# Strided sparse attention with a multiplicative feed-forward: q and k transposes in 64-row halves, joined with the scores of the pair before

## The chip, the cores and the metric

The kernel runs on one core of one Trainium2 chip. The metric is the device time of one execution in microseconds. TensorE (PE) does matmuls and transposes, VectorE (DVE) and ScalarE (ACT) read their results out of PSUM and do the elementwise work, GpSimd (POOL) casts loaded data, SyncE (SP) issues loads.

## The reference, cut to what matters

Eight batches, eight heads, 576 positions, head width 64. Heads 0 to 3 look at the last 32 positions, heads 4 to 7 at all earlier positions that are equal modulo 32. The attention's output, 4608 tokens of 512, goes through a feed-forward with no activation function: two products multiplied with each other, then two more matrices.

```python
scores = scale * np.matmul(q, k.transpose(0, 1, 3, 2))
mask_local = (rel >= 0) & (rel < stride)                       # stride = 32
mask_strided = (rel >= 0) & (pos[None, :] % stride == pos[:, None] % stride)
attn = np.exp(scores - max); attn = attn / (sum + 1e-09)        # masked scores count as nothing
x = np.matmul(attn, v)            # -> 4608 x 512
h = (x @ w1) * (x @ w2) @ w3      # 512 -> 1024 -> 1024
out = h @ w_out                   # 1024 -> 512
```

## The kernel before, in words

**Feed-forward.** w3 and w_out are folded once into one matrix `w34` (`fold_tr` transposes w3 on TensorE, `fold_mm` multiplies). Tokens then go in nine chunks of 512. A chunk has 16 units of four 512-column matmuls in `ab_halves` (`a` fills `aps`, which ACT copies to `asb`; `bb` fills `bps`, which DVE multiplies with `asb` into `abt`) and eight units in `o_halves` (two units per output tile; ACT copies it to `osb` and issues the store). Their outputs take turns on the three buffers of `psF`.

**Attention.** Work goes by pairs of heads, four pairs per batch: `hp` 0 and 1 are local (six chunks of 96 queries), `hp` 2 and 3 strided (eight chunks of 72). The phases of a pair are:

- `ph_T` (L208): eight 128x128 transposes of q and k into one `psM` tile, then one copy into `qT` (always ACT) and one into `kT` (ACT in the first two batches, DVE after that). The two copies read different halves of the tile. Positions 512 to 575 are done for all pairs of a batch at once in `ph_R` (L225), with four transposes and four small copies.
- `ph_S` (L238): two halves of a pair's chunks. Each half has 6 or 8 score matmuls, which alternate between the heads (array rows 0 to 63 and 64 to 127) and write the two halves of a `psB` tile; then exp on ACT (L253) over 576 columns and the mask product on DVE (L255).
- `ph_PV` (L259): for each half 6 or 8 matmuls with v into another `psB` tile. v carries a column of ones, so column 65 of each chunk is the sum of the exps; DVE takes its reciprocal (L274) and multiplies (L276).
- `ph_T2` (L279): six or eight transposes back into a `psM` tile, and a copy into `xT` (ACT, or DVE for local pairs from batch 2 on), from which the feed-forward reads.

**PSUM.** `psF` has 3 buffers, `psB` 2 of double size, `psM` 1, and all eight banks are taken.

**Order.** TensorE's instructions keep the order in which the code writes them (`pe`, L65). The Tile framework derives all waits between the engines from the order in the code, and orders the instructions of the other engines itself. The attention phases are put in a list (`stream`, L377 to L397), and `host` (L400) sets them between the units of the weight fold or of a feed-forward chunk, evenly: batch 0 goes into the fold, batch 1 into the first chunk, batch b into chunk b-1. With the order of before, a batch in the middle has 21 such items among 24 units. `batch_end` marks where a batch must be complete, because the next chunk reads its `xT`.

Loads of q, k and v are issued on SP's queue one to two chunks ahead and cast by POOL (L74, L181, L192).

Of the kernel before, what the change touches and what calls it, by code (L numbers as in the profile page):

```python
# [8 lines left out]
FP32 = mybir.dt.float32  # L9
FP16 = mybir.dt.float16  # L10
AF = mybir.ActivationFunctionType
# [3 lines left out]
def _ap(t: bass.AP, off_add, dims):  # L15
    return bass.AP(tensor=t.tensor, offset=t.offset + off_add, ap=dims)
# [3 lines left out]
def kernel(  # L20
# [11 lines left out]
    nc = tc.nc  # L32
    B, H, S, D = q.shape
# [3 lines left out]
    P = 128  # L37
# [4 lines left out]
    scale = 1.0 / float(D) ** 0.5  # L42
# [6 lines left out]
    SQ, ST = 72, 8  # L49
    NM = 512  # L50
    NR = S - NM
    KW = 640

    consts = ctx.enter_context(tc.tile_pool(name="consts", bufs=1))
    stgp = ctx.enter_context(tc.tile_pool(name="stgp", bufs=9))
    qkp = ctx.enter_context(tc.tile_pool(name="qkp", bufs=2))
    att = ctx.enter_context(tc.tile_pool(name="att", bufs=2))
    ffn = ctx.enter_context(tc.tile_pool(name="ffn", bufs=2))
    psF = ctx.enter_context(tc.tile_pool(name="psF", bufs=3, space=bass.MemoryType.PSUM))
    psB = ctx.enter_context(tc.tile_pool(name="psB", bufs=2, space=bass.MemoryType.PSUM))  # L60
    psM = ctx.enter_context(tc.tile_pool(name="psM", bufs=1, space=bass.MemoryType.PSUM))

    AHEAD = 2

    def pe(ins):  # L65
        return tc.keep_in_program_order(ins)

    def copy(eng, out, in_):
        if eng == "a":
            nc.scalar.copy(out=out, in_=in_)  # L70
        elif eng == "v":
            nc.vector.tensor_copy(out=out, in_=in_)  # L72
        else:
            nc.gpsimd.tensor_copy(out=out, in_=in_)  # L74


    id16 = consts.tile([P, P], FP16)
# [3 lines left out]
    maskL = consts.tile([P, LQ], FP16)  # L81
# [16 lines left out]
    maskS = consts.tile([SQ, SQ], FP16)  # L98
# [9 lines left out]

    qT = consts.tile([P, 4, S], FP16)
    kT = consts.tile([P, 4, KW], FP16)  # L110
    ptms = [consts.tile([P, 640], FP16, name=f"ptm{i}") for i in range(4)]
    nc.vector.memset(kT[:, 0:2, 0:32], 0.0)
    nc.vector.memset(kT[:, 2:4, S:KW], 0.0)
    for i in range(2):
        nc.vector.memset(v16L[i][:, :, :, D], 1.0)
        nc.vector.memset(v16L[i][0:32, :, 0, :], 0.0)
        nc.vector.memset(v16S[i][:, :, :, D], 1.0)
    for i in range(4):
        nc.vector.memset(ptms[i][:, 576:640], 0.0)

    xT = [consts.tile([P, NTOK], FP16, name=f"xT{cc}") for cc in range(4)]
    w1h = consts.tile([P, KM, DF], FP16)
# [31 lines left out]
    x16 = {}  # L154
# [43 lines left out]
    pairs = []  # L198
    for b in range(B):
        for hp in range(4):  # L200
            s = Pair()
            s.b, s.hp, s.local = b, hp, hp < 2
            s.w, s.n = (LQ, LT) if s.local else (SQ, ST)
            s.kr = P if s.local else SQ
            s.ptm, s.xqs = {}, {}
            pairs.append(s)

    def ph_T(s):  # L208
        ps = psM.tile([P, 2, NM], FP16, tag="m")
        for i, nm in enumerate("qk"):  # L210
            src = x16[(s.b, nm, s.hp // 2)]
            h0 = 2 * (s.hp % 2)
            for c in range(4):
                pe(nc.tensor.transpose(ps[:, i, c * P:(c + 1) * P],  # L214
                                       src[:, c, h0:h0 + 2].rearrange("p h d -> p (h d)"), id16))
        for i, (eng, t) in enumerate((("a", qT), ("a" if s.b < AHEAD else "v", kT))):
            if s.local:
                c0 = 32 * i
                copy(eng, t[:, s.hp, c0:c0 + NM].rearrange("x (p c) -> x p c", c=4),
                     ps[:, i].rearrange("x (c p) -> x p c", c=4))  # L220
            else:
                copy(eng, t[:, s.hp, 0:S].rearrange("x (u c w) -> x u c w", u=2, c=4)[:, :, :, 0:64],
                     ps[:, i].rearrange("x (c t u) -> x u c t", c=4, u=2))

    def ph_R(b):  # L225
        ps = psM.tile([P, 4, 2, 128], FP16, tag="m")
        pv = ps.rearrange("x g a w -> x (g a w)")[:, 0:512].rearrange("x (g a w) -> x g a w", g=4, a=2)
        src = x16[(b, "r")]
        for g in range(4):
            pe(nc.tensor.transpose(pv[:, g].rearrange("x a w -> x (a w)"),  # L230
                                   src[:, 2 * g:2 * g + 2].rearrange("p h d -> p (h d)"), id16))
        for i, (eng, t) in enumerate((("a", qT), ("a" if b < AHEAD else "v", kT))):
            c0 = 32 * i + NM
            copy(eng, t[:, 0:2, c0:c0 + NR], pv[:, 0:2, i])
            copy(eng, t[:, 2:4, 0:S].rearrange("x g (c w) -> x g c w", w=SQ)[:, :, :, 64:SQ],
                 pv[:, 2:4, i].rearrange("x g (s c) -> x g c s", c=ST))

    def ph_S(s):  # L238
        w, kr = s.w, s.kr
        m = s.n // 2  # L240
        for g in range(2):
            sps = psB.tile([P, 2, 512], FP32, tag="big")
            for i in range(m):
                t = g * m + i
                ks = w * t
                for h in range(2):
                    r = bass.ds(64 * h, 64)
                    pe(nc.tensor.matmul(sps[:, h, i * w:(i + 1) * w], kT[r, s.hp, ks:ks + P],  # L248
                                        qT[r, s.hp, ks:ks + w], start=True, stop=True))
            pte = att.tile([P, 2, 288], FP16, tag="pte", bufs=3)  # L250
            ptm = ptms[(2 * s.hp + g) % 4]
            s.ptm[g] = ptm
            nc.scalar.activation(out=pte[0:kr], in_=sps[0:kr, :, 0:288], func=AF.Exp, bias=0.0, scale=scale)  # L253
            mk = maskL if s.local else maskS
            nc.vector.tensor_mul(ptm[0:kr, 0:576].rearrange("p (a x) -> p a x", x=w),  # L255
                                 pte[0:kr].rearrange("p h (a x) -> p (h a) x", x=w),
                                 _ap(mk, 0, [[mk.ap[0][0], kr], [0, s.n], [1, w]]))

    def ph_PV(s, g):  # L259
        w, kr = s.w, s.kr  # L260
        m = s.n // 2
        ptm = s.ptm[g]
        vt = (v16L if s.local else v16S)[s.b % 2]
        xps = psB.tile([P, 2, 512], FP32, tag="big")
        for i in range(m):
            for h in range(2):
                c0 = h * 288 + i * w
                pe(nc.tensor.matmul(xps[:, h, i * 65:(i + 1) * 65], ptm[0:kr, c0:c0 + P],  # L268
                                    vt[0:kr, 2 * (s.hp % 2) + h, g * m + i, :], start=True, stop=True))
        rcp = att.tile([P, 2, 4], FP32, tag="rcp")  # L270
        xqs = att.tile([P, 4, 2, D], FP16, tag="xqs", bufs=4)
        s.xqs[g] = xqs
        xv = xps[0:w, :, 0:m * 65].rearrange("p h (i e) -> p h i e", e=65)
        nc.vector.reciprocal(out=rcp[0:w, :, 0:m], in_=xv[:, :, :, D])  # L274
        rp = rcp.ap[0][0]
        nc.vector.tensor_mul(xqs[0:w, 0:m].rearrange("p i h d -> p h i d"), xv[:, :, :, 0:D],  # L276
                             _ap(rcp, 0, [[rp, w], [4, 2], [1, m], [0, D]]))

    def ph_T2(s):  # L279
        w, n = s.w, s.n  # L280
        m = n // 2
        ps = psM.tile([P, 1024], FP16, tag="m")
        for t in range(n):
            pe(nc.tensor.transpose(ps[:, t * w:(t + 1) * w],  # L284
                                   s.xqs[t // m][0:w, t % m].rearrange("p h d -> p (h d)"),
                                   id16[0:w, 0:w]))
        o = xT[s.hp][:, S * s.b:S * s.b + S]
        if s.local:
            copy("a" if s.b < AHEAD else "v", o, ps[:, 0:S])
        else:  # L290
            nc.scalar.copy(out=o.rearrange("x (p c) -> x p c", c=n),  # L291
                           in_=ps[:, 0:S].rearrange("x (c p) -> x p c", p=w))
# [78 lines left out]
    stream = []  # L371
    batch_end = {}

    def add(f, *a):
        stream.append(lambda: f(*a))

    for b in range(B):  # L377
        if b < AHEAD:
            add(ph_T, pairs[4 * b])
            add(ph_R, b)  # L380
            add(ph_T, pairs[4 * b + 1])
        for i in range(4):
            p = 4 * b + i
            add(ph_S, pairs[p])
            if i or b >= AHEAD:
                add(ph_T2, pairs[p - 1])
                if i == 0:
                    batch_end[b - 1] = len(stream)
            add(ph_PV, pairs[p], 0)
            if i == 3 and AHEAD <= b + 1 < B:  # L390
                add(ph_R, b + 1)
            add(ph_PV, pairs[p], 1)
            if i < 2 or AHEAD <= b + 1 < B:
                add(ph_T, pairs[p + 2])
        if b + 1 < AHEAD or b == B - 1:
            add(ph_T2, pairs[4 * b + 3])
            batch_end[b] = len(stream)  # L397
    pos = [0]

# [38 lines left out]
    for jc in range(KF):  # L438
        h0, h1 = fold_mm(jc)
# [59 lines left out]
```

## Time and profile before

| what | value |
|---|---|
| three runs | 295.0, 295.15, 292.44 us, median 295.0 |
| profiled execution | span 299.8 us, from the first to the last instruction; no other time of it is given |
| TensorE clock granted, mean | 0.989 |
| DMA | 48.64 MB, mean 162 GB/s |
| weight fold with batch 0 | about 22 to 49 us |
| chunk 0 with batch 1 | about 49 to 85 us |
| chunks 1 to 6 with batches 2 to 7 | about 85 to 249 us |
| chunks 7 and 8, no attention beside | to the end |

How to read the profile: a line of the timeline has the start, the length, the engine, the line of the code, the operation, `out<-in`, the shapes and the number of instructions that were merged. Matmuls overlap one another, so what a group takes from TensorE is read from its start to the start of the next group; the length also holds the last matmul's own passage. In square brackets stands the time for which the engine was idle ahead of the line and what ended it. A line of the waits has who waited for whom, the total in us, how many times, and the longest.

### The profile page before, as it was taken

Reading aid. Unit: us, or ns where it says so; the run is one execution under the profiler, and the core shown is the slowest. Engines: PE = TensorE matmul, PEld = TensorE weight load, DVE = VectorE, ACT = ScalarE, POOL = GpSimd, SP = SyncE. Lnnn points to the kernel's source line nnn. Section 1 sums busy time; section 2 is a strip of 40 time slices with the busy share of each in tenths; the row PEclk is TensorE's granted clock in tenths of the full one; section 3 lists DMA queues with packets and bytes.
Section 4 is the critical chain, followed back from the end, with each engine's and each line's share of the span. In section 5 each row is a group of like instructions: output and inputs, shape, how many; then the busy total and the mean of one; then the engine's idle time right before and its main releaser. Section 6 shows DMA issues by size and latency. Waiting matters only on the chain.

```text
span 299.8 us, 6132 instructions
## 1 busy us (share of the span) xinstructions
PE 268.9 (90%) x2401; PEld 141.6 (47%) x2401; DVE 174.6 (58%) x353; ACT 147.1 (49%) x269; POOL 102.1 (34%) x118
## 2 busy tenths in 40 slices
PE   2258898989889989989999899999999999999995
PEld 1025554435545545545555445555555555444442
DVE  2011775357888866886789659747765774340430
ACT  2025586557565545536645554564455445333332
POOL 5539744486626724653455345110000000000000
PEclk9996999999999999999999999999999999999999
DMA  7999999999869929994896796030012002003003
GB/s 228 349 160 352 288 348 258 216 273 209 249 200 243 242 79 270 246 178 159 240 236 140 253 193 164 27 115 2 2 57 87 0 2 105 35 2 116 24 2 140
DMA packets 58653, 48.64 MB, mean 162 GB/s; under 512 B 29184, under 2 KB 49664, under 8 KB 58624
## 3 DMA queue, kind: packets, MB, share of 16 engines
q1 hardware_dynamic: 53440, 38.81, 54.7%
q10 hardware_dynamic: 5184, 9.44, 8.7%
q8 instruction: 19, 0.31, 0.5%
q14 instruction: 10, 0.08, 0.1%
HBM read 38.80 MB, written 9.44 MB: 161 GB/s over the span
## 4 chain that ended last, share of the span: by engine, by line
PE 67%; DVE 9%; DMA 9%; ACT 9%; issue 3%; SPq 1%; POOL 0%; ACTq 0%
PE ops L335 19%; PE bps L321 18%; PE aps L312 16%; PE xps L268 4%; PE ps L214 4%; DMA st<-in_moe_w_dram 4%; ACT pte L253 3%; DVE ptm L255 3%; DMA st<-in_moe_w_out_dram 3%; DMA out_dram<-osb 3%; PE sps L248 2%; PE ps L284 2%; DVE abt L323 2%; ACT xT L291 2%; DVE kT L72 2%
## 5 line engine op out<-in xcount | busy, mean ns | idle before, releaser
L312 PE MATMUL aps<-xT,w1h 128*128 128x512 f16 x288 | 75.3, 379 | 3.2 <-ACT xT L291 3.0
L323 DVE TENSOR_TENSOR abt<-bps,asb 128x512 f16<-128x512 f32 x72 | 49.5, 687 | 47.2 <-PE bps L321 45.5
L321 PE MATMUL bps<-xT,w2h 128*128 128x512 f16 x288 | 74.0, 379 | 0.0
L315 ACT COPY asb<-aps 128x512 f32<-128x512 f32 x72 | 42.2, 586 | 64.6 <-PE aps L312 61.8
L335 PE MATMUL ops<-w,abt 128*128 128x512 f16 x288 | 71.7, 379 | 0.5 <-DVE abt L323 0.5
L74 POOL CAST t<-st 128x1024 f16<-128x1024 f32 (+1 forms) x48 | 47.4, 991 | 43.4 <-DMA st<-in_k_dram 29.1
L253 ACT ACTIVATE pte<-sps 128x576 f16<-128x576 f32 (+1 forms) x64 | 38.4, 650 | 7.3 <-PE sps L248 7.1
L276 DVE TENSOR_TENSOR xqs<-xps,rcp 96x384 f16<-96x384 f32 (+1 forms) x64 | 39.6, 619 | 2.0
L321 PEld LDWEIGHTS <-w2h 128*128 128x128 f16 x288 | 25.8, 97 | 31.6 <-issue 5.1
L70 ACT COPY qT<-ps 128x512 f16<-128x512 f16 (+1 forms) x48 | 22.9, 481 | 29.9 <-PE ps L214 23.8
L346 ACT COPY osb<-ops 128x512 f32<-128x512 f32 x36 | 21.1, 586 | 29.9 <-PE ops L335 28.6
L335 PEld LDWEIGHTS <-abt 128*128 128x128 f16 x288 | 24.7, 98 | 23.1 <-DVE abt L323 1.0
L312 PEld LDWEIGHTS <-w1h 128*128 128x128 f16 x288 | 25.1, 98 | 22.2
L181 POOL CAST v16L<-st 32x768 f16<-32x768 f32 (+1 forms) x32 | 27.1, 847 | 18.4 <-DMA st<-in_v_dram 12.6
L268 PEld LDWEIGHTS <-ptm 72*128 72x128 f16 (+1 forms) x448 | 21.4, 97 | 19.2 <-DVE ptm L255 6.4
L255 DVE TENSOR_TENSOR ptm<-pte,maskL 128x576 f16<-128x576 f16 x32 | 20.5, 646 | 11.7 <-ACT pte L253 11.2
L72 DVE COPY kT<-ps 128x512 f16<-128x512 f16 (+1 forms) x36 | 18.8, 535 | 10.1 <-ACT qT L70 10.0
L255 DVE TENSOR_TENSOR ptm<-pte,maskS 72x576 f16<-72x576 f16 x32 | 19.6, 620 | 8.5 <-ACT pte L253 7.9
L192 POOL CAST v16S<-st 72x1024 f16<-72x1024 f32 x16 | 16.9, 1055 | 20.1 <-PE xps L268 11.4
L335 PE MATMUL ops<-woh,w3T 128*128 128x512 f16 x64 | 19.8, 440 | 3.2 <-POOL woh L74 3.1
L214 PEld LDWEIGHTS <-t 128*128 128x128 f16 x256 | 17.1, 99 | 8.8 <-issue 2.6
L214 PE MATMUL ps<-id,t 128*128 128x128 f16 x256 | 20.1, 222 | 0.5 <-POOL t L74 0.5
(48 smaller groups left out, 175.8 us busy)
## 6 DMA issues: line engine op xcount, KB each, us to landing
out_dram<-osb ACTq DMA_DIRECT2D x36, 256.0 KB, 2.0
st<-in_moe_w_dram SPq DMA_DIRECT2D x16, 512.0 KB, 8.9
st<-in_q_dram SPq DMA_DIRECT2D x16, 512.0 KB, 5.5
st<-in_k_dram SPq DMA_DIRECT2D x16, 512.0 KB, 6.6
st<-in_v_dram SPq DMA_DIRECT2D x32, 144.0 KB, 6.1
st<-in_v_dram SPq DMA_DIRECT2D x16, 256.0 KB, 7.2
st<-in_moe_w_out_dram SPq DMA_DIRECT2D x4, 512.0 KB, 8.5
st<-in_q_dram SPq DMA_DIRECT2D x8, 128.0 KB, 8.1
```

The source lines that it names most:

```text
L74: nc.gpsimd.tensor_copy(out=out, in_=in_)
L181: nc.gpsimd.tensor_copy(out=vt[pr, hs, :, 0:D], in_=st[pr])
L214: pe(nc.tensor.transpose(ps[:, i, c * P:(c + 1) * P], src[:, c, h0:h0 + 2].rearrange("p h d -> p (h d)"), id16))
L253: nc.scalar.activation(out=pte[0:kr], in_=sps[0:kr, :, 0:288], func=AF.Exp, bias=0.0, scale=scale)
L255: nc.vector.tensor_mul(ptm[0:kr, 0:576].rearrange("p (a x) -> p a x", x=w), pte[0:kr].rearrange("p h (a x) -> p (h a) x", x=w), _ap(mk, 0, ...
L268: pe(nc.tensor.matmul(xps[:, h, i * 65:(i + 1) * 65], ptm[0:kr, c0:c0 + P], vt[0:kr, 2 * (s.hp % 2) + h, g * m + i, :], start=True, stop=T ...
L276: nc.vector.tensor_mul(xqs[0:w, 0:m].rearrange("p i h d -> p h i d"), xv[:, :, :, 0:D], _ap(rcp, 0, [[rp, w], [4, 2], [1, m], [0, D]]))
L312: pe(nc.tensor.matmul(aps, w1h[:, ci, bass.ds(jc * P, P)], xT[ci][:, tok], start=(ci == 0), stop=(ci == KM - 1)))
L315: nc.scalar.copy(out=asb, in_=aps)
L321: pe(nc.tensor.matmul(bps, w2h[:, ci, bass.ds(jc * P, P)], xT[ci][:, tok], start=(ci == 0), stop=(ci == KM - 1)))
L323: nc.vector.tensor_mul(abts[tch][:, jc, :], bps, st["asb"])
L335: pe(nc.tensor.matmul(st["ps"], lhs(ci), rhs(ci), start=(ci == 0), stop=(ci == KF - 1)))
```

## The change

- The transposes of q and k become 16 instead of 8, each of 64 rows: the halves of the rows (`u`) alternate and write the two halves of a tile `pt`. The 64 last positions (`rest`), once per batch, are eight further transposes in the same tile; `ph_R` is gone.
- A new phase `ph_TS` (the block) writes the transposes of the next pair, its q and k copies, then all scores of the present pair, then the copies of the rest.
- The scores go into one tile `sps` (columns 0 to 511 of each half), except for the last chunk of each head, which goes into columns 384 and up of `pt`, beside the transposes. The first score of a block in the code is that of head 0's last chunk.
- exp and mask run once over what lies in `sps` (2 x 480 or 2 x 504 columns) and once over what lies in `pt` (2 x 96 or 2 x 72).
- PV has groups of three chunks: two groups for local pairs, three (3, 3, 2) for strided ones. All but the last write into the halves of `sps`; the last takes a `psM` tile.
- Strided pairs' q and k copies are split by the half of the tile.
- `psB` (4 banks) is replaced by `psA` and `psT`, one buffer of 2 banks each. `psM` serves T2 and the last PV group.
- A batch in the middle now has 18 items among the 24 units: (block, T2, PV0, PV1) twice and (block, T2, PV0, PV1, PV2) twice.

```diff
+    NB = 512
+    LC = 384
-    psB = ctx.enter_context(tc.tile_pool(name="psB", bufs=2, space=bass.MemoryType.PSUM))
+    psA = ctx.enter_context(tc.tile_pool(name="psA", bufs=1, space=bass.MemoryType.PSUM))
+    psT = ctx.enter_context(tc.tile_pool(name="psT", bufs=1, space=bass.MemoryType.PSUM))
...
+            s.n1 = NB // s.w
+            s.groups = [list(range(g, min(g + 3, s.n))) for g in range(0, s.n, 3)]
...
+    def ph_T(s, rest, pt):
+        ps = pt.bitcast(FP16)
+        h0 = 2 * (s.hp % 2)
         for i, nm in enumerate("qk"):
             src = x16[(s.b, nm, s.hp // 2)]
             for c in range(4):
+                c0 = i * 256 + c * 64
+                for u in range(2):
+                    r = half_rows(u)
+                    pe(nc.tensor.transpose(ps[:, u, c0:c0 + 64],
+                                           src[r, c, h0:h0 + 2].rearrange("p h d -> p (h d)"), id16[r, r]))
+        if rest:
...
+        engs = (("a", qT), ("a" if s.b < AHEAD else "v", kT))
+        for i, (eng, t) in enumerate(engs):
+            pi = ps[:, :, i * 256:i * 256 + 256]
             if s.local:
                 c0 = 32 * i
+                copy(eng, t[:, s.hp, c0:c0 + NM].rearrange("x (u p c) -> x u p c", u=2, c=4),
+                     pi.rearrange("x u (c p) -> x u p c", c=4))
             else:
+                to = t[:, s.hp, 0:S].rearrange("x (v c w) -> x v c w", v=2, c=4)
+                for u in range(2):
+                    copy(eng, to[:, :, :, 32 * u:32 * u + 32],
+                         pi[:, u].rearrange("x (c t v) -> x v c t", c=4, v=2))
...
+    def ph_S(s, pt):
+        w, kr, n, n1 = s.w, s.kr, s.n, s.n1
+        sps = psA.tile([P, 2, NB], FP32, tag="a", name="sps")
+        s.ps = sps
+
+        def sc(h, c):
+            r = half_rows(h)
+            o = sps[:, h, c * w:(c + 1) * w] if c < n1 else pt[:, h, LC:LC + w]
+            pe(nc.tensor.matmul(o, kT[r, s.hp, w * c:w * c + P], qT[r, s.hp, w * c:w * c + w],
+                                start=True, stop=True))
+
+        for i in range(n):
+            sc(0, (i - 1) % n)
+            sc(1, i)
+        pte = att.tile([P, 2 * S], FP16, tag="pte", bufs=2)
+        ptm = s.ptm = ptms[s.hp % 2]
+        mk = maskL if s.local else maskS
+        m1 = 2 * n1 * w
+        for lo, hi, src in ((0, m1, sps[0:kr, 0:2, 0:n1 * w]), (m1, 2 * S, pt[0:kr, :, LC:LC + w])):
+            nc.scalar.activation(out=pte[0:kr, lo:hi], in_=src, func=AF.Exp, bias=0.0, scale=scale)
+            nc.vector.tensor_mul(ptm[0:kr, lo:hi].rearrange("p (a x) -> p a x", x=w),
...
+        if g < len(s.groups) - 1:
+            xps = s.ps[:, g]
+        else:
+            pv2 = psM.tile([P, NB], FP32, tag="m", name="pv2")
+            xps = pv2[:, :]
...
+    def ph_TS(t, s):
+        pt = psT.tile([P, 2, NB], FP32, tag="t")
+        after = ph_T(t, t.hp == 0, pt) if t is not None else (lambda: None)
+        if s is not None:
+            ph_S(s, pt)
+        after()
+
+    for p, s in enumerate(pairs):
+        b, i = divmod(p, 4)
+        if i == 0 and b < AHEAD:
+            add(ph_TS, s, None)
+        nxt = pairs[p + 1] if p + 1 < len(pairs) else None
+        if nxt is not None and nxt.hp == 0 and nxt.b < AHEAD:
+            nxt = None
+        add(ph_TS, nxt, s)
+        if i or b >= AHEAD:
+            add(ph_T2, pairs[p - 1])
...
+        for g in range(len(s.groups)):
+            add(ph_PV, s, g)
+        if i == 3 and (b + 1 < AHEAD or b == B - 1):
+            add(ph_T2, s)
             batch_end[b] = len(stream)
```

## The prediction

> **What bounds the kernel now.** I read the page first (engines, clock, chain), then the stages, the order of time around one pair, and last the waits.
>
> ```profile
> span 299.8 us, 6132 instructions
> PE 268.9 (90%) x2401; PEld 141.6 (47%) x2401; DVE 174.6 (58%) x353; ACT 147.1 (49%) x269; POOL 102.1 (34%) x118
> PE 67%; DVE 9%; DMA 9%; ACT 9%; issue 3%; SPq 1%; POOL 0%; ACTq 0%
> ```
>
> TensorE is the bound: 67% of the chain that ended last. Busy time alone says less, so the stages:
>
> ```profile
> 22.40:49.20 26.80, 23.30 (x268) 14.60 (x269) 15.88 (x35) 18.27 (x34) 17.58 (x18) 0.89 1.06 324
> 66.80:84.50 17.70, 15.27 (x200) 8.87 (x197) 13.74 (x29) 11.83 (x24) 10.20 (x11) 1.00 0.97 216
> 190.60:218.50 27.90, 27.60 (x275) 14.94 (x272) 18.49 (x41) 15.15 (x28) 1.04 (x1) 1.00 0.11 39
> ```
>
> The columns are PE, PEld, DVE, ACT and POOL busy, then the clock. From about 84 us on PE leaves almost nothing (27.60 of 27.90); there a change is worth what it adds to or takes from PE's own queue. At 22 to 49 us (batch 0 beside the weight fold) and 58 to 84 us (batch 1) PE waits for the chain score, exp, mask, PV. One local pair of the dense part, PE, ACT and DVE in turn:
>
> ```profile
> 204.32 0.61 PE L214 MATMUL ps<-id,t 128*128 128x128 f16 x8
> 204.77 1.03 PE L312 MATMUL aps<-xT,w1h 128*128 128x512 f16 x4
> 205.73 0.43 PE L248 MATMUL sps<-qT,kT 64*128 64x96 f16 x12
> 206.09 1.04 PE L321 MATMUL bps<-xT,w2h 128*128 128x512 f16 x4
> ...
> 204.97 0.58 ACT L70 COPY qT<-ps 128x512 f16<-128x512 f16 x1 [0.91 <-PE ps L214]
> 205.59 0.69 DVE L72 COPY kT<-ps 128x512 f16<-128x512 f16 x1 [0.30 <-ACT qT L70]
> ```
>
> PE time is read from start to start: T 0.45 us, scores 0.36, and 0.09 before them (204.77 + 0.864 for the unit of four matmuls ahead is 205.64). The kT copy starts only when the qT copy ends, though the two read different halves of `ps`. The waits say that this is the rule:
>
> ```profile
> DVE kT L72 <- ACT qT L70: 10.0, 19, 1.2
> ACT w3T L360 <- DVE w3T L359: 15.9, 5, 8.7
> PE ps L284 <- DVE kT L72: 2.2, 4, 1.0
> ```
>
> In the first two lines engines take turns on one PSUM tile while reading disjoint columns. So the program orders users of such a tile by place, not by bytes. In the third, T2 waits for T's copies, as both use `psM`.
>
> **The change, part by part.** A unit is four 512-column matmuls, 0.864 us by the starts above 51 us (51.17, 52.03, 52.90). Let e be the end of the unit ahead of a block.
>
> *Transposes.* 8 of 128 columns took 0.45. How 64-row halves run is shown by the scores, which already alternate halves: 16 of 72 columns take 0.43 including 0.20 of the last one's own time, so 15.6 ns each; 64 columns should do no worse, 16 x 14.5 = 0.23. I take 0.23; if the halves did not overlap, 16 x 29 = 0.47. Gain 0.22 per pair. R (4 of 128, 0.225) becomes 4 more pairs, 0.117. The 0.09 and some 0.1 behind the scores are paid once either way. The Trainium skill (TensorE: Matmul & The Clock Gate, Wait — 56ns, not 53.3ns?) gives a floor of about 25 ns from start to start for small matmuls; by it T would take 0.40 and 30 blocks 5 us more. This trace disagrees, with 15.6 ns.
>
> *The new wait, which decides.* `pt` holds the transposes and the last score chunk in the same two halves, other columns. In the code the q and k copies come before the scores, PE keeps its written order, and the first score written, `sc(0, n-1)`, goes into `pt`. By the rule seen above it waits for both copies. Behind it on PE stand all scores and the next units; ACT's exp, DVE's mask and PV wait in turn. Today nothing waits so: T writes for a pair that comes later and a unit fills the gap.
> Local, k on DVE: from the first T matmul to the end of kT were 206.28 - 204.32 = 1.96 (other pairs 1.95 to 2.0); T ends 0.17 sooner (last start 0.39 to 0.22), so 1.79. PE resumes 0.05 later (84.43 after a copy that ended at 84.38). So scores start at e + 0.09 + 1.84 = e + 1.93, and the next unit 0.36 later at e + 2.29. Before: 0.45 + 0.09 + 0.36 = 0.90. Cost **1.38** net of the gain; with R's move, 0.117 - 0.225, **1.27**.
> Strided: copies are split by half. ACT 128x512 is 587 ns, 128x128 269, so 256 columns 375; DVE 689 and 228, so 382. From T's start: q0 0.48 to 0.855, k0 0.89 to 1.27, k1 to 1.65. The first score needs half 0 only (1.32), the last half 1 (1.70): next unit at e + 1.92, cost **1.01**; if it waits for all copies, 1.24. No row shows which; the code's order (h=0 tail first, h=1 tail last) fits the first, so I take 1.01.
> The Trainium skill (PSUM — Partial Sum Buffer, PSUM bank collisions raise a hardware error) tells one to guard PSUM by bank and quadrant, not by address. The kT and w3T waits agree; guarded by address, the sum would be that of the third rival.
>
> *exp and mask.* exp 657 ns for 576 columns; at the copies' 0.83 ns a column 976 and 338 for 960 and 192, the same in all, but the first part ends 0.32 later. Mask (mean 646, quiet 0.45, crowded 1.06 at 64.01) by width: 1.08 (0.75 to 1.77). PV0 is ready at scores + 0.34 + 0.98 + 0.05 + 1.08 = 2.45. In the dense part 18 items now share 24 units (21 before): three units and a T2 stand between, 0.36 + 2.59 + 0.26 = 3.2, hidden; behind the first strided pair only two, 2.35 against 2.6 with its later second half: 0.25 x 6 batches = **1.5** (0 to 5).
>
> *T2 of the last pair* sits behind one unit; its xT copy queues on ACT behind both exps and an osb: scores + 2.75, against PE's fourth aps matmul at 2.13: 0.6 for today's 0.30, five times: **1.5**.
>
> *Third PV group, split copies.* Strided pairs get one more reciprocal and product (recip. 3 x 0.18 for 2 x 0.20; products 0.554 twice + 0.423 for 2 x 0.685: 0.29) and split copies (ACT 0.16, DVE 0.08): 16 x 0.37 = 6 us on DVE, 3 on ACT. DVE is at 18.5 of 27.9: hidden, 0 to 1.
>
> *PSUM.* T leaves `psM`, so T2 no longer waits for kT: **-2.2**, 1.04 of it inside batch 1. Single `psA`: the next scores come over two units after the last PV that writes there: 0. R moves some 3.5 us ahead; its cast was ready (batch 4's at 131.7, scores at 133.97). No DMA moves; SP's and POOL's order stays.
>
> *Batches 0 and 1.* Here PE already waits and the items stand one unit apart, so I walk the chain by hand with the same terms. The cycle from pair 1 to pair 2 in batch 0: block begins 33.7; T done and copies on ACT from 34.15 (before batch 2 kT is copied there too, parts 0.27 apart); k0 ends 35.05, scores 35.1 to 35.45; exp after the last copy 35.65 to 36.6; mask with POOL beside it 1.2 and a little ahead of it, 38.0; PV0, a unit, PV1, a unit; next block 40.3, scores 41.7: 6.6 us. Before, the halves followed each other and the copies were done in the gaps: 33.81 to 39.52, 5.7. Walked so, the scores of pairs 0 to 3 start at 29.2, 35.1, 41.7, 47.7 (before 28.64, 33.81, 39.52, 43.65), and the batch ends at 53.3 for 49.2: **+4.1**. Bounds +1 (the wait falls wholly into time in which PE waits) and +7 (it adds wholly, with longer masks).
> Batch 1, from T at 58.08 to the first aps behind its T2 at 84.68, was 26.6. After, from the same point: a lone T block with the rest, whose six ACT copies hold the single `psT` until 2.4; T 2.5, scores of pair 4 at 4.05, of 5 at 10.95, of 6 at 17.0, of 7 at 24.4 (R's transposes in it), pair 8's block ends 31.7, T2 32.0: **+5.4**, pair 8's wait included. Bounds +2 and +8, by the same reasons.
>
> **Sum.** Pairs 9 to 30: 5 local at 1.38, 12 strided at 1.01, 5 with R at 1.27 = 25.4. With 1.5 + 1.5 - 1.2 = 27.2. With 4.1 + 5.4: +36.7. The profiled execution is shown only as its span, 299.8, 4.8 over the median 295.0 of the runs; I add to the median: **332 us**. Bounds: low, nothing for PV0 and xT and +3 for both early batches, 295 + 25.4 - 1.2 + 3 = 322; high, split copies waited for whole (12 x 0.23 = 2.8), PV0 +5 and early batches +15: 295 + 25.4 + 2.8 + 5 + 1.5 - 1.2 + 15 = 343.
>
> **Rivals.**
> - *Copies start late.* When T is done ACT may be in an asb or osb copy (197.33: qT only at 197.81) or DVE in abt; 0.48 in half of the 30 blocks is +7: 339; in all of them with whole-tile waits, 350. Against: units ahead of the blocks are mostly bps, which leave ACT free. 0.12.
> - *Halves don't overlap.* 30 x 0.24 = +7: 339. Against: scores. 0.08.
> - *No wait* (other side). If the scores into `pt` do not wait, T and R give 30 x 0.22 + 7 x 0.11 = 7.4 and psM 2.2; the early batches cost 3.5 and the strided PV0 and xT 4, as exp stands behind the copies: 295 - 9.6 + 7.5 = 293. It decides where the wait per block is under 0.3 us. For it: no row shows a matmul held by a reader of other columns. Against: kT and w3T, 24 waits in all, none seen to overlap. 0.08.
> - *Early batches absorb it.* Their +9.5 falls to 0, as PE waits there anyway: 322. Against: the wait lies on their chain too. 0.10.
> My forecast 0.62, 322 to 343 by itself.
>
> **How the numbers follow.** The likeliest is 332. The range 318 to 345 holds it, the early-batch case and most of the two at 339, leaving out the no-wait case and the 350 end: about 0.15. About 1% is what a measurement of this kernel can tell from no change. Only the no-wait case is not slower: half of it (0.04) faster by over 1%, half (0.04) within 1%, the rest 0.92 slower.
>
> **What would show it.** PE's scores waiting for DVE kT (ACT kT in the first two batches), 1 to 1.5 us each, 30 times; one batch of the dense part 32 to 33 us for 27.9, PE busy nearer 0.85; transposes at about 15 ns from start to start; T2's wait on kT gone; xT's wait about doubled. It is wrong if scores start within 0.2 us of the last transpose.

## The result, and the profile after

The changed kernel takes 349.8 us (median of four runs, 347.5 to 350.3) against 295.1: a ratio of 1.184, interval 1.177 to 1.192. Times of a kernel are medians of its fast runs from here on; runs more than 1.5% above the fastest of the same kernel are left out. I had forecast 332 with a range of 318 to 345. The direction and the cause were right, the size was not: +54.7 us where the sum had +36.7.

The page of the changed kernel: span, engines, granted clock by slice, chain.

```profile
span 348.5 us, 6789 instructions
PE 274.6 (79%) x2689; PEld 138.5 (40%) x2689; DVE 170.3 (49%) x395; ACT 148.8 (43%) x289; POOL 101.1 (29%) x118
PEclk9998999879989999989989999999999999999999
PE 63%; ACT 12%; DVE 9%; DMA 7%; issue 6%; POOL 1%; SPq 1%; ACTq 0%; DVEq 0%
```

PE's share fell from 90% to 79%, no other engine's share rose, and ACT's share of the chain rose from 9% to 12%: the added time is PE waiting. PEclk has more eights than before, which becomes important below. The waits name what PE waits for:

```profile
PE pt L267 <- DVE kT L76: 37.5, 24, 2.1
PE pt L267 <- ACT kT L74: 7.5, 6, 1.3
PE sps L297 <- DVE xqs L305: 2.8, 5, 1.1
```

24 + 6 = 30 waits, one for each block that has transposes and scores, 45.0 us together. The line `PE ps <- DVE kT` of before is gone, as forecast. One block in a quiet stretch, with the transposes and copies of a strided pair:

```profile
242.89 0.41 PE L226 MATMUL pt<-id,t 64*128 64x64 f16 x16
...
243.34 0.65 ACT L74 COPY qT<-pt 128x256 f16<-128x256 f16 x2 [0.81 <-PE pt L226]
244.02 0.76 DVE L76 COPY kT<-pt 128x256 f16<-128x256 f16 x2 [0.26 <-ACT qT L74]
...
244.83 0.21 PE L267 MATMUL pt<-qT,kT 64*128 64x96 f16 x1 [1.53 <-DVE kT L76]
244.83 0.42 PE L267 MATMUL sps<-qT,kT 64*128 64x96 f16 x10
...
245.19 1.04 PE L340 MATMUL aps<-xT,w1h 128*128 128x512 f16 x4
```

Read downward: the 16 transposes, both q copies, then both k copies, and only after the end of the second of them (244.77) the first score. DVE had nothing else to do: it stood idle for 0.26 us and took the first k copy at 244.02, after the end of the second q copy (243.98) and not after that of the first (243.71). From first transpose to first score 1.94 us, of which PE idles 1.53.

A second profile of the kernel before (the run e0, below) had a span of 295.4; stage by stage, by the starts of the first `aps` of each chunk:

| stage | before (e0) | after | difference | forecast |
|---|---|---|---|---|
| to chunk 0 (fold, batch 0) | 46.4 | 53.1 | +6.8 | +4.1, end at 53.3 |
| chunk 0 (batch 1) | 36.1 | 45.0 | +8.9 | +5.4 |
| chunks 1 to 6 (batches 2 to 7) | 167.5 | 204.8 | +37.3 | +27.2 |
| chunks 7 and 8 | 45.4 | 45.5 | +0.1 | 0 |

### The profile page after: what moved, and what is told of

It reads as the page before. It is cut to its first block, busy times and chain, and to the rows that moved or that the text cites. A ratio compares the mean times of both kernels' runs of the same rounds, so it can differ in the third digit from the quotient of the medians.

```text
span 348.5 us, 6789 instructions
## 1 busy us (share of the span) xinstructions
PE 274.6 (79%) x2689; PEld 138.5 (40%) x2689; DVE 170.3 (49%) x395; ACT 148.8 (43%) x289; POOL 101.1 (29%) x118
## 3 DMA queue, kind: packets, MB, share of 16 engines
q1 hardware_dynamic: 53440, 38.81, 45.5%
## 4 chain that ended last, share of the span: by engine, by line
PE 63%; ACT 12%; DVE 9%; DMA 7%; issue 6%; POOL 1%; SPq 1%; ACTq 0%; DVEq 0%
PE bps L349 18%; PE aps L340 17%; PE ops L363 16%; DVE kT L76 5%; ACT qT L74 4%; DMA st<-in_moe_w_dram 3%; PE sps L297 3%; ACT pte L278 2%; PE pt L226 2%; DMA st<-in_moe_w_out_dram 2%; PE pt L267 2%; PE sps L267 2%; DVE ptm L279 2%; PE ps L312 2%; ACT kT L74 1%
## 5 line engine op out<-in xcount | busy, mean ns | idle before, releaser
L349 PE MATMUL bps<-xT,w2h 128*128 128x512 f16 x288 | 77.5, 393 | 0.0
L351 DVE TENSOR_TENSOR abt<-bps,asb 128x512 f16<-128x512 f32 x72 | 49.7, 690 | 54.7 <-PE bps L349 53.7
L78 POOL CAST t<-st 128x1024 f16<-128x1024 f32 (+1 forms) x48 | 47.0, 986 | 43.6 <-DMA st<-in_k_dram 27.7
L267 PE MATMUL pt<-qT,kT 64*128 64x96 f16 (+1 forms) x64 | 12.8, 199 | 45.0 <-DVE kT L76 37.5
L278 ACT ACTIVATE pte<-sps 128x960 f16<-128x960 f32 (+1 forms) x32 | 31.7, 989 | 34.9 <-PE pt L267 34.5
L297 PEld LDWEIGHTS <-ptm 72*128 72x128 f16 (+1 forms) x448 | 24.4, 100 | 28.8 <-DVE ptm L279 8.3
L74 ACT COPY qT<-pt 128x256 f16<-128x256 f16 (+2 forms) x64 | 23.2, 403 | 22.4 <-PE pt L226 16.5
L267 PEld LDWEIGHTS <-kT 64*128 64x128 f16 x448 | 11.2, 95 | 49.1 <-issue 26.7
L279 DVE TENSOR_TENSOR ptm<-pte,maskL 128x960 f16<-128x960 f16 (+1 forms) x32 | 15.4, 523 | 29.8 <-ACT pte L278 29.8
L279 DVE TENSOR_TENSOR ptm<-pte,maskS 72x1008 f16<-72x1008 f16 (+1 forms) x32 | 16.3, 543 | 23.3 <-ACT pte L278 23.0
L305 DVE TENSOR_TENSOR xqs<-sps,rcp 72x384 f16<-72x384 f32 (+1 forms) x48 | 26.6, 554 | 1.6
L76 DVE COPY kT<-pt 128x256 f16<-128x256 f16 (+2 forms) x48 | 19.8, 441 | 13.0 <-ACT qT L74 13.0
```

The costliest lines, as they stand in the source:

```text
L267: pe(nc.tensor.matmul(o, kT[r, s.hp, w * c:w * c + P], qT[r, s.hp, w * c:w * c + w], start=True, stop=True))
L278: nc.scalar.activation(out=pte[0:kr, lo:hi], in_=src, func=AF.Exp, bias=0.0, scale=scale)
L279: nc.vector.tensor_mul(ptm[0:kr, lo:hi].rearrange("p (a x) -> p a x", x=w), pte[0:kr, lo:hi].rearrange("p (a x) -> p a x", x=w), _ap(mk, 0 ...
L297: pe(nc.tensor.matmul(xps[:, o0:o0 + 65], s.ptm[0:kr, c0:c0 + P], vt[0:kr, 2 * (s.hp % 2) + h, c, :], start=True, stop=True))
L349: pe(nc.tensor.matmul(bps, w2h[:, ci, bass.ds(jc * P, P)], xT[ci][:, tok], start=(ci == 0), stop=(ci == KM - 1)))
L351: nc.vector.tensor_mul(abts[tch][:, jc, :], bps, st["asb"])
```

## The experiments

**e0_before_again**: the kernel before, with no edit, for its profile.

> The kernel of before, unchanged, for a second profile: the first had a span of 299.8 us while its four runs took 292.4 to 296.6. If that profiled execution was itself a long one (a 1.77 us wait of PE for xT behind a store at 171 us), this one should have a span of 291 to 296 and no such wait. If profiling lengthens the span, it is again near 300.

It ran in 297.1 us with a span of 295.4, so an execution's time is its span and 1.7 us. The first profile of before (299.8) was therefore an execution of some 301.5 us, longer than any of the runs; batch 0 ended in it at 49.2, here at 46.4. PE's longest wait for xT is 1.4 us here, for 1.8 there.

**e1_copies_last**: the change, with the q and k copies written behind the scores.

```diff
+        def qk_out():
             for i, (eng, t) in enumerate(engs):
...
         def rest_out():
+            qk_out()
...
-        return rest_out if rest else (lambda: None)
+        return rest_out if rest else qk_out
```

> The change with the q and k copies written behind the scores, nothing else moved. Theory (the scores' writes into pt wait for the copies that read pt): the 45 us for which PE stood idle ahead of the scores (37.5 until DVE kT, 7.5 until ACT kT) go, and with them most half-clock stretches (5 to 7 us); exp no longer stands behind the copies. 293 to 302 us, no wait of scores for kT in the profile. Rival (the large exp and mask, the single psA and the third PV group make it slower, and the wait is only where it shows): still over 325, with PE waiting for masks or xqs instead.

306.3 us (305.7 to 308.8; 308.8 is also the median of all five runs), ratio to before 1.033 (1.027 to 1.040). The place of two copies in the code is worth 43.6 of the 54.7 us. No score waits for kT any more. The time stayed above the 293 to 302 expected, and PE shows two other waits, of which the first grew from the 2.8 us of the changed kernel:

```profile
PE sps L299 <- DVE xqs L307: 10.9, 14, 3.1
PE aps L342 <- ACT xT L321: 6.8, 8, 1.7
```

PV's second group for strided pairs writes half 1 of `sps` and waits until DVE has read the first group out of half 0. I had put the single `psA` at zero.

**e2_tails_last**: the change, with the scores in plain order, so that both scores that go into `pt` come last.

```diff
         for i in range(n):
-            sc(0, (i - 1) % n)
+            sc(0, i)
             sc(1, i)
```

> The change with the scores in plain order, so that both scores that go into pt are the last two of a block instead of the first and the last. Theory (only a write into pt waits): the other 10 or 14 scores start within 0.3 us of the last transpose, only the last two wait, as long as before minus some 0.2 us; 30 blocks x 0.2 = 6 us: 341 to 347. Rival (scores wait because copies write qT and kT, which they read): the first score waits as before and the time stays at 348 to 351.

334.9 us (333.3 to 337.7), ratio 1.132 (1.124 to 1.141), 14.9 us less. A block with a strided pair's copies:

```profile
207.03 0.41 PE L226 MATMUL pt<-id,t 64*128 64x64 f16 x16
...
207.28 0.39 PE L267 MATMUL sps<-qT,kT 64*128 64x72 f16 x14
...
208.97 0.21 PE L267 MATMUL pt<-qT,kT 64*128 64x72 f16 x2 [1.30 <-DVE kT L76]
```

14 scores read `qT` and `kT` while the copies write other parts of them, and start 0.25 us after the first transpose; only the two that write into `pt` wait. That settles the place of the wait. The gain was more than twice what I expected. An undisturbed chunk fell from 33.9 to 32.9, that is 0.25 in each of four blocks. The two profiled executions differ by 12.5 us (348.5 and 336.0): 7.8 in chunks 1 to 6, of which 22 x 0.25 = 5.5 are the blocks; 4.1 in chunk 0; 0.6 in batch 0. In chunks 0 to 6 the halved clock, of which more below, comes in two stretches of 3.4 us where the change has five.

**e3_full_rows_q_k_apart**: the change with full transposes, q into half 0 of `pt` and k into half 1, one copy each.

```diff
-                c0 = i * 256 + c * 64
-                for u in range(2):
...
+                pe(nc.tensor.transpose(ps[:, i, c * P:(c + 1) * P],
+                                       src[:, c, h0:h0 + 2].rearrange("p h d -> p (h d)"), id16))
...
-            pi = ps[:, :, i * 256:i * 256 + 256]
+            pi = ps[:, i, 0:NM]
```

> The change with the 8 full 128-row transposes of before instead of the 16 halves, q into half 0 of pt and k into half 1, and single copies, still ahead of the scores. If users take turns by half (bank) of the tile, kT on DVE no longer waits for qT: from the first transpose to the scores about 1.4 us instead of 1.84 and 1.94, some 0.5 us in each of 23 blocks: 338 to 343. If they take turns by the whole tile: first transpose to scores about 2.1, 0.2 us more in each of 30 blocks: 352 to 357.

346.3 us (341.8 to 346.9), ratio 1.165 (1.155 to 1.175), between the two forecasts, so its time decides little. Its rows decide:

```profile
226.51 0.61 PE L223 MATMUL pt<-id,t 128*128 128x128 f16 x8
...
227.16 0.58 ACT L74 COPY qT<-pt 128x512 f16<-128x512 f16 x1 [0.85 <-PE pt L223]
227.77 0.69 DVE L76 COPY kT<-pt 128x512 f16<-128x512 f16 x1 [1.29 <-ACT qT L74]
228.52 0.20 PE L262 MATMUL pt<-qT,kT 64*128 64x96 f16 x1 [1.40 <-DVE kT L76]
```

DVE stands idle for 1.29 us, and kT still starts behind the end of qT (227.74), though the two now read different halves of the tile. So users take turns by the whole tile. From first transpose to score 2.01 us, as the second theory had it (about 2.1). That the time did not rise fits the clock: the profiled execution (341.8 us) has no stretch of halved clock in chunks 1 to 6, where that of the change has three, and takes 201.6 us there for 204.8, though its quiet chunk is longer (34.1 for 33.9).

**e4_copies_last_two_psA**: e1, with the scores in two tiles, one per head, and the large exp as two instructions.

```diff
-    psA = ctx.enter_context(tc.tile_pool(name="psA", bufs=1, space=bass.MemoryType.PSUM))
+    psA = ctx.enter_context(tc.tile_pool(name="psA", bufs=2, space=bass.MemoryType.PSUM))
...
-        sps = psA.tile([P, 2, NB], FP32, tag="a", name="sps")
-        s.ps = sps
+        sps = s.ps = [psA.tile([P, NB], FP32, tag="a", name=f"sps{h}") for h in range(2)]
...
```

> The change with the copies behind the scores (308.8 us in the run before) and, besides, psA as two separate tiles, one for each head, so that exp of the large part is two instructions again. Theory (users take turns by whole tile, so PV's second group waits until DVE has read the first one's half): the 10.9 us of PE waiting for DVE xqs go; ACT has 32 more fixed costs of some 0.16 us, off the path: 297 to 303 us. Rival (the second group is late for its masks anyway): the wait moves to DVE ptm and the time stays at 306 to 310.

298.1 us (294.8 to 299.1), ratio 1.005 (1.000 to 1.010), 8.1 us less than e1 (10.0 by the spans of the profiled executions, 307.0 and 297.0), for a wait of 10.9. As much memory and the same columns: what counts as one tile has changed, and that exp is two instructions. PE's wait of a second PV group for DVE xqs is no longer among the waits; the scores wait for xqs 1.6 us in two places.

**e5_copies_behind_T2**: e4, with the q and k copies one item later, behind T2's copy.

```diff
+    def ph_T2c(s, cur):
+        ph_T2(s)
+        cur.after()
...
-            add(ph_T2, pairs[p - 1])
+            add(ph_T2c, pairs[p - 1], s)
```

> As e4_copies_last_two_psA, with the q and k copies one item later, behind T2's copy. Theory (the 6.8 us of aps waiting for ACT's xT copy are the q copy and both exps that stand ahead of it on ACT): the wait falls from 0.9 to about 0.4 us in each of six chunks, and kT no longer stands ahead of masks and xT on DVE: 3 to 5 us under e4, 292 to 299. Rival (the exps alone make xT late): within 1 us of e4.

296.4 us (293.0 to 297.4; 297.0 over all ten runs), ratio 1.000 (0.995 to 1.006): level with before. The wait of `aps` for xT fell in the quiet chunks from 0.94 to 0.44 us, as expected. The time fell by 1.7 us and not by 3 to 5, and even that cannot be told from the spread of the two kernels.

**e6_change_with_filled_wait**: the change, with 16 matmuls of the identity, which compute nothing that is used, between transposes and scores.

```diff
+                fill = psF.tile([P, 512], FP32, tag="f", name="fill")
+                for i in range(16):
+                    pe(nc.tensor.matmul(fill[:, 0:P], id16, id16, start=True, stop=True))
             ph_S(s, pt)
```

> The change with 16 matmuls of the identity (128 columns, some 0.9 us) between the transposes and the scores of each of the 30 blocks, into a psF buffer that nobody reads: work that computes nothing, put into time in which PE waits for the copies. Theory (part of what my sum lacked is the TensorE clock: 4 half-clock stretches of 3.4 us more than before, brought on by the idle time): PE is no longer idle for long, the clock stays at 0.985 or more, and the time falls by 3 to 8 us, 342 to 347, though work was added. Rival (the clock drops come from elsewhere or cost nothing): clock 0.97 and the time stays at 349 to 352 or rises.

341.5 us (340.2 to 344.2), ratio 1.150 (1.141 to 1.159): 8.3 us less than the change, with 480 matmuls more. The clock of the profiled execution:

```profile
core 0: 340.0 us, clock 0.995
```

It is 0.969 in the changed kernel. The blocks themselves did not become shorter: from first transpose to first score the 22 of chunks 1 to 6 take 43.2 us together in the change and 43.1 here. So PE's idle time cost twice: itself, and the clock behind it.

**e7_masks_per_head**: e5, with the large mask also as one instruction per head.

```diff
-        for lo, hi in ((0, m1), (m1, 2 * S)):
+        for lo, hi in ((0, m1 // 2), (m1 // 2, m1), (m1, 2 * S)):
```

> As e5_copies_behind_T2 (297.0 us), with the large mask also as two instructions, one per head, so that the first runs beside the second exp. Theory (what is left of PE's waits for DVE ptm, 7.8 us in 11 places, is the one large mask that starts only when both exps are done): PV's first group is ready some 0.25 to 0.5 us sooner; 293 to 296 us. Rival (those waits are POOL slowing DVE, or lie in the early batches behind other work): within 1 us of 297.

295.4 us (293.0 to 296.8), ratio 0.997 (0.994 to 1.001): not told apart from before, nor surely from e5. The waits for masks went from 7.8 us in 11 places to 6.8 in 7. In chunks 1 to 6 they fell from 1.1 to 0.2; all the others lie in the early batches, as the rival had it. By stage this last kernel differs from before even so: its profiled execution takes 163.4 us for chunks 1 to 6 where e0 takes 167.5, and 84.7 for 82.5 up to there.

**e8_full_rows_without_the_wait**: e5 with the 8 full transposes in place of the 16 halves (the transposes and single copies as in e3).

> As e5_copies_behind_T2, with the 8 full 128-row transposes of before in place of the 16 halves and single copies for strided pairs. It measures the gain of the halves by itself, where nothing waits behind them. By my term, 0.21 to 0.22 us in each of 30 blocks: 6.5 us more than e5, 302 to 305, and in the profile 0.45 us from the first transpose to the next group instead of 0.24. If the gain is lost in waits elsewhere: within 2 us of 297.

297.6 us (295.7 to 299.95), ratio 1.007 (1.002 to 1.011). One block here, and one of e5:

```profile
209.19 0.61 PE L223 MATMUL pt<-id,t 128*128 128x128 f16 x8
209.73 0.43 PE L263 MATMUL sps<-qT,kT 64*128 64x72 f16 x14
```

```profile
207.56 0.41 PE L226 MATMUL pt<-id,t 64*128 64x64 f16 x16
207.80 0.42 PE L268 MATMUL sps<-qT,kT 64*128 64x72 f16 x14
```

Here 8 transposes and the change to half rows take 0.54 us to the next group, where the 16 halves of e5 take 0.24 and the change to half rows, 0.09 us, stands ahead of them: 0.21 a block, my term. A quiet chunk takes 27.9 us against 27.04 in e5, four times 0.21; but the medians are only 1.2 apart, not 6.5, and the intervals of the two ratios overlap. The gain is seen in the quiet chunks and not shown in the whole time.

## Why the prediction was wrong in size and right in cause

**Right: the step that decides.** "The new wait, which decides" named the place (the first score into `pt`), what ends it (kT on DVE, on ACT in the first two batches) and the count of 30. e2 shows the place, e1 the price. Local blocks were forecast at 1.84 us from first transpose to first score and measured 1.81 (235.10 to 236.91); with the rest 1.96 and 1.93 (225.73 to 227.66). The transposes took 0.24 us for 16, forecast 0.23. Batch 0's end, walked by hand, was 53.3 and is 53.1; that it fits so well is luck, as the account below shows.

**Wrong: the strided block, "cost 1.01; if it waits for all copies, 1.24".** I let users take turns by half of the tile, on the ground that the order of the tails fitted it; even the other end let k's first half start behind q's first. By whole tile both k copies wait for both q copies: 1.94 us to the first score where I had 1.32, and 2.41 from the end of the unit ahead to the next unit (217.28 to 219.69) where I had 1.92. Twelve blocks in chunks 1 to 6: 0.49 x 12 = 5.9 us. The rows of before showed turns inside one buffer of `psM`, a single bank, so they could not tell bank from tile; but nothing in them spoke for halves. e3 shows the whole tile directly.

**Wrong: copies that start late.** In six of the twelve strided blocks of chunks 1 to 6 a copy was late: in four DVE was held by a copy of v or a product (145.85 to 148.21 is 2.36 us), in two ACT by an `asb` copy (2.08 and 2.09). Together 1.2 us over the 1.94. This was part of the first rival, at a smaller price; that the rival's far end, 350, is the measured time is chance, as it took some 14 us for late copies.

**Missing: the clock.** No term had it: I priced PE's idle time at its own length. The profile has it in the windows and in the matmuls; here the four full chunks from 98 us on and, by the order of time, one block after a wait of 1.95 us:

```profile
98.10:133.10 35.00, 28.94 (x312) 14.55 (x310) 22.73 (x50) 15.61 (x31) 17.99 (x20) 0.95 0.89 198
133.10:168.90 35.80, 29.11 (x314) 14.97 (x311) 20.61 (x49) 15.45 (x31) 12.85 (x14) 0.95 0.85 205
168.90:204.50 35.60, 29.14 (x315) 14.91 (x312) 19.86 (x49) 15.46 (x31) 10.05 (x11) 0.95 0.52 139
204.50:238.40 33.90, 27.44 (x314) 14.28 (x311) 19.83 (x49) 15.32 (x31) 7.41 (x8) 1.00 0.09 32
```

```profile
148.21 0.20 PE L267 MATMUL pt<-qT,kT 64*128 64x72 f16 x1 [1.95 <-DVE kT L76]
...
148.57 1.35 PE L340 MATMUL aps<-xT,w1h 128*128 128x512 f16 x4
149.72 0.68 PE L312 MATMUL ps<-id,xqs 96*128 96x96 f16 x6
150.21 1.91 PE L349 MATMUL bps<-xT,w2h 128*128 128x512 f16 x4
151.91 0.54 PE L297 MATMUL sps<-v16S,ptm 72*128 72x65 f16 x6
```

The unit at 150.21 takes 1.70 us to the next start, about twice 0.864. Chunks with a clock of 0.95 are 1.1 to 1.9 us longer than the one with 1.00. e6 prices it: 3.3 us less in chunks 1 to 6 (201.5 for 204.8), 3.1 in chunk 0, 2.2 in batch 0.

**The account.** Chunks 1 to 6 missed 10.1 us: 5.9 for the strided blocks, 1.2 for late copies, 3.3 for the clock, less 0.2 in the other blocks, which were a little shorter than forecast. The remaining terms came to about the +1.8 that they were given, but that sum is luck: PE's waits outside the blocks fell from 3.3 us (e0) to 2.8 there, where PV0 and xT were to raise them. Chunk 0 missed 3.5: 3.1 for the clock; the rest I cannot split, but one copy came late there too (ACT took an `osb` copy first, and the block at 94.98 needed 2.46 us to its first score). Batch 0 missed 2.7 against e0, though its end was met: the profile of before that I worked from had that end 2.8 us late, and the walk left out the clock, 2.2 us by e6. The two nearly cancel.

**Smaller steps.** xT: forecast 0.6 us a chunk, measured 0.40; the forecast had the order on ACT right and the times a little long. PV0: forecast 1.5 us, while waits of PV for masks in chunks 1 to 6 are 0.3 us. Single `psA` at zero: 2.8 us in the changed kernel and, with the large wait taken away, 8 us (e4 against e1), hidden until then behind the first one. The halves' gain is real (e8) and lies inside a block that lost seven times as much. The rival "no wait" is refuted; its 293 for a kernel without the wait would have been too low for the same reason, since e1 has 306.3.

## What to carry to other kernels

Before two uses are put into one PSUM tile, list who reads and writes it in the order of the code: engines took turns on the whole tile, even on disjoint columns and halves, and a matmul that writes beside data still being read stops everything behind it on TensorE. Moving the readers behind it in the code, and then cutting another such tile in two of half the size, removed 44 and 8 us without changing any arithmetic. On a TensorE that is nearly full, an idle gap can cost more than its length, through the clock; and when one wait is removed, look for the one that it covered.

## What the runs showed of the hardware

- TensorE's clock was halved in stretches of 3.41 us that lie on a grid of the same period: in the changed kernel they begin at 29.7, 67.2, 70.7, 98.0, 149.2 and 176.5 us, all whole multiples of 3.41 apart. What counted was TensorE's idle time within one window of that grid, not the length of a gap. Three pairs of neighbouring windows:

```profile
145.74:149.16 3.42, 1.47 (x36) 0.91 (x36) 2.51 (x5) 1.13 (x3) 2.35 (x3) 1.00 1.10 273
149.16:152.57 3.41, 3.41 (x20) 1.70 (x18) 1.54 (x4) 1.29 (x3) 0.00 (x0) 0.50 1.30 210
173.05:176.46 3.41, 1.70 (x34) 0.88 (x32) 2.19 (x5) 1.12 (x4) 1.35 (x2) 1.00 1.22 291
176.46:179.88 3.42, 3.42 (x15) 1.54 (x13) 1.61 (x4) 1.32 (x3) 0.00 (x0) 0.50 0.48 64
111.61:115.02 3.41, 1.72 (x37) 0.91 (x36) 2.37 (x6) 1.31 (x4) 1.32 (x2) 1.00 1.40 153
115.02:118.44 3.42, 3.42 (x30) 1.72 (x28) 2.55 (x6) 1.76 (x4) 2.20 (x3) 1.00 1.18 219
```

  Idle time is a window's length less PE's busy time, the first number behind the comma. Behind 1.95 and 1.71 us of it the clock is 0.50, behind 1.69 it stays at 1.00: the line lies at half a window. A gap of 1.71 us (209.40 to 211.11) that fell across two windows, 1.20 and 0.51, did nothing. In the eleven profiles, from 24 us to shortly before the end, each such stretch that begins at full clock stands behind a window with 1.71 us idle or more, and no window with less has one behind it; one window (60.70 in e7, 1.84 us) should have had one by this and has none. Before 24 us it does not hold (19.45 in the changed kernel: 2.81 us idle, and none). This is read from the traces; no run shifted a gap against the grid. The Trainium skill (TensorE: Matmul & The Clock Gate, HAM oscillation — how this bites in real kernels) gives idle gaps of over about 3.4 us as the rule; here gaps of 1.71 to 2.05 us were enough, in three of six chunks.
- Work that computes nothing made a kernel 8.3 us faster, by keeping the clock up (e6): the only stretch of halved clock left before its last matmuls begins at 20.1 us.
- 64-row transposes that alternate between the two halves of the array's rows ran at 15 ns from start to start (16 in 0.24 us), 0.53 of the 0.45 us of 8 full ones.
